# Another order of the seven half-size products in a fused sigmoid-attention and gated feed-forward kernel, with a second relu buffer and transposes in single banks

## The chip, the cores and the metric

The kernel runs on one core of a Trainium2 chip. The metric is the device time of one execution in microseconds (us), the median of several. A core has a matrix engine (TensorE, "PE" in the profile, with its weight loads shown apart as "PEld"), three engines for elementwise work (VectorE "DVE", ScalarE "ACT", GpSimd "POOL"), and DMA queues ("SPq" is the one that SyncE issues). TensorE writes its results to PSUM, here eight banks of 512 fp32 values for each of 128 partitions. This kernel uses four of the banks as two "pairs" (for attention) and four as single "banks" (for the feed-forward part).

## The reference, cut to what matters

```python
# q, k, v: (8, 12, 448, 64) fp32     w_gate, w_val: (768, 1536)     w_out: (1536, 768)
scores = q @ k.T / 8 - log(448)
attn   = sigmoid(scores) @ v                        # no softmax: each score alone
x      = attn, heads side by side                   # (3584 tokens, 768)
out    = (relu(x @ w_gate) * (x @ w_val)) @ w_out   # (3584, 768) fp32
```

There are 8 batches of 448 tokens. The kernel works on the feed-forward part of batch b and, woven into it, on the attention of batch b+1.

## The kernel before

For batches 1 to 7 the three matrix products are done by Winograd's form of Strassen's method: a product of 2 x 2 blocks costs seven block products in place of eight. For a group g of two feature blocks (six groups a batch) the products are numbered k = 1 to 7. Product 1, 2 and 4 take the tokens as they are (`xT`), products 3, 5, 6 and 7 take sums of token blocks (`S`); some of the weights are differences prepared before (`Tw`; for 7 the top half of `wv`, overwritten by a difference). One product is six matmuls of 128 x 128 by 128 x 224.

The seven products are put together in three banks: b1 holds 1, then adds 2; b2 holds 6, then adds 5, then adds 3; b3 holds 7, then adds 4. Between the products of one bank another engine reads what is there so far. A matmul that adds to a bank must therefore wait until the reader of the previous state is done.

```python
BANK = {1: "b1", 2: "b1", 6: "b2", 5: "b2", 3: "b2", 7: "b3", 4: "b3"}

def product(key, k, matmuls):
    first = k in (1, 6, 7)
    if first:
        live[key, BANK[k]] = take()            # the bank that was given back longest ago
    bank = banks[live[key, BANK[k]]]
    for i, (c0, c1, lhsT, rhs, last) in enumerate(matmuls):
        nc.tensor.matmul(bank[:, c0:c1], lhsT, rhs, start=(first and i == 0), stop=last, ...)

def tmp(key, nm):                              # s1, s2, s4: two buffers each; r1: one
    live[key, nm] = tmpp.tile([P, S], FP32, tag=nm, name=nm, bufs=1 if nm == "r1" else 2)
    return live[key, nm]

def gv_product(b, g, k):
    # ... the six matmuls, then, with ps = the bank:
    if k == 1:
        nc.scalar.copy(tmp(key, "s1")[:], ps)
    elif k == 6:
        add(tmp(key, "s2")[:], ps, live[key, "s1"][:])
    elif k == 5:
        t = tmp(key, "s4")
        add(t[:], ps, live[key, "s1"][:])
        add(t[:], banks[live[key, "b3"]][:, 0:S], t[:])
    elif k == 2:
        nc.scalar.activation(tmp(key, "r1")[:], ps, AF.Relu)
        give(i)
    elif k == 3:
        t = live[key, "s1"]
        add(t[:], ps, t[:])
        give(i)
        nc.gpsimd.tensor_tensor(out=out[:, :, o : o + HS], in0=two(live[key, "r1"]), in1=two(t), op=AOP.mult)
    elif k == 4:
        t = live[key, "s2"]
        add(t[:], ps, t[:])
        give(i)
        nc.vector.scalar_tensor_tensor(out=out[:, :, o + HS : o + S], in0=two(t), scalar=0.0,
            in1=two(live[key, "s4"]), op0=AOP.max, op1=AOP.mult)
```

`add` and `subtract` are VectorE `tensor_tensor` instructions. `out` is the activation tile `hT`. The last matrix product (`out_product`) works in the same way on pairs of token blocks (six matmuls of 128 x 384), with `hT` and sums of it as stationary operand. `sums(("h", pair), ks)` and `sums(("x", b), ks)` make the sums `S` on VectorE.

The order in which the products are emitted is a list; each engine executes its own instructions in the order of emission:

```python
def ffn(b):
    p, o = 4 * (b - 1), 4 * (b - 1) + 2        # the two pairs of output blocks of this turn
    todo = gv((0, 1)) if b == 1 else []        # each entry is (group, k)
    todo += gv((0, 7), (0, 2), (0, 6), (1, 1), (0, 5), (1, 6), (0, 3), (0, 4), (1, 7), (1, 5), (1, 2), (2, 1), (1, 3))
    for g in range(2, HFC):                    # HFC = 6
        todo += gv((g, 6), (g - 1, 4), (g, 7), (g, 5), (g, 2))
        todo += gv((g + 1, 1)) if g + 1 < HFC else [("out", p, 1)] if b > 1 else []
        todo += gv((g, 3))
    todo += gv((HFC - 1, 4))
    # ... then the output products; "plain" (b == 1) is an ordinary product of two token blocks
    # behind[...]: sums emitted straight after an entry
```

Attention is woven in by "visits": `scores(n, c)` makes two banks of a pair (four matmuls of 64 x 64 by 64 x 448), ScalarE turns them into one `PT` tile by a sigmoid, and `values(n, ...)` multiplies the seven `PT` tiles of a block of four heads by v. A visit is two scores, or score, values, score. The list `due` gives the times, counted in matmul time of the list, after which the next visit is emitted.

```python
PTp = ctx.enter_context(tc.tile_pool(name="PTp", bufs=9))

def transposes(n, nm, *engines, cut=(0, NCH)):
    if n <= NBLK:                              # NBLK = 3 blocks a batch, NCH = 7 chunks a block
        bank = take(); tr = banks[bank][:, 0:S]
    else:
        bank = None; tr = next_pair()[:, 0, 0:S]
    # ... seven PE transposes into tr, a copy to qT or kT, give(bank) if it was a bank

due = dues(0.5 if b > 1 else 1.5, total - 4.2) if b + 1 < B else []
```

On GpSimd run, in this order before batch 1: the casts of q, k and v of coming blocks, of the gate and value weights, and (as their DMAs land) of the twelve parts of `w_out` (`wo`).

Of the kernel before, what the change touches and what calls it, by code (L numbers as in the profile page):

```python
# [9 lines left out]
FP32 = mybir.dt.float32  # L10
FP16 = mybir.dt.float16
# [5 lines left out]
def kernel(  # L17
# [33 lines left out]
    h16p = ctx.enter_context(tc.tile_pool(name="h16p", bufs=3))  # L51
    v16p = ctx.enter_context(tc.tile_pool(name="v16p", bufs=3))
    qkTp = ctx.enter_context(tc.tile_pool(name="qkTp", bufs=4))
    PTp = ctx.enter_context(tc.tile_pool(name="PTp", bufs=9))
    xTp = ctx.enter_context(tc.tile_pool(name="xTp", bufs=4))
    sxp = ctx.enter_context(tc.tile_pool(name="sxp", bufs=1))
    tmpp = ctx.enter_context(tc.tile_pool(name="tmpp", bufs=2))
# [9 lines left out]
    def next_pair():  # L67
        turn["pair"] ^= 1
        return pairs[turn["pair"]]

    def take():

        return free.pop(0)

    def give(i):
        free.append(i)
# [98 lines left out]

    def transposes(n: int, nm: str, *engines, cut=(0, NCH)):
        h16 = qk16.pop((nm, n))
        if n <= NBLK:
            bank = take()
            tr = banks[bank][:, 0:S]  # L180
        else:
            bank = None
            tr = next_pair()[:, 0, 0:S]
        tr = tr.bitcast(FP16).rearrange("p (c h k) -> p c h k", c=NCH, h=2)
        for c in range(cut[0], cut[-1]):
            nc.tensor.transpose(tr[:, c], h16[:, c, :, :], ident[:])
        t2 = qkT.get((nm, n)) or qkTp.tile([P, NCH, 2, KC], FP16, tag="qkT", name=f"{nm}T")
        for c0, c1, eng in zip(cut, cut[1:], engines or (nc.vector,)):
            if eng is nc.scalar:
                eng.copy(t2[:, c0:c1], tr[:, c0:c1])  # L190
            else:
                eng.tensor_copy(t2[:, c0:c1], tr[:, c0:c1])
        if bank is not None:
            give(bank)
        qkT[nm, n] = t2

    def scores(n: int, c: int):
# [122 lines left out]
    def add(out, a, b):  # L320
        nc.vector.tensor_tensor(out=out, in0=a, in1=b, op=AOP.add)  # L321
# [69 lines left out]
    live: dict = {}  # L391

    def tmp(key, nm):
        live[key, nm] = tmpp.tile([P, S], FP32, tag=nm, name=nm, bufs=1 if nm == "r1" else 2)
        return live[key, nm]

    BANK = {1: "b1", 2: "b1", 6: "b2", 5: "b2", 3: "b2", 7: "b3", 4: "b3"}
# [12 lines left out]
    def gv_product(b: int, g: int, k: int):  # L410

        key = ("gv", b, g)
        h, kh = {1: (0, 0), 2: (0, 1), 4: (1, 1)}.get(k, (None, None))
        if h is None:
            a = [S_[("x", b), {3: 4, 5: 1, 6: 2, 7: 3}[k]][:, dc] for dc in range(HDC)]
        else:
            a = [xT[b, kh][:, dc, h * HS : (h + 1) * HS] for dc in range(HDC)]

        def w(j, dc):
            if k in (1, 2):  # L420
                return wg[j][:, (k - 1) * HDC + dc]
            if k == 3:
                return wv[j][:, HDC + dc]
            return T[{4: 4, 5: 1, 6: 2, 7: 3}[k], j][:, dc]

        mm = []
        for fi in range(2):
            j, jj = divmod(2 * g + fi, FG)
            for dc in range(HDC):
                mm.append((fi * HS, (fi + 1) * HS, w(j, dc)[:, jj * P : (jj + 1) * P], a[dc], dc == HDC - 1))  # L430
        product(key, k, mm)
        i = live[key, BANK[k]]
        ps = banks[i][:, 0:S]
        o = (b % NHALF) * S
        out = hT[:, 2 * g : 2 * g + 2]

        def two(t):
            return t[:].rearrange("p (f s) -> p f s", f=2)
# [5 lines that stand above are left out]
        elif k == 5:  # L444
            t = tmp(key, "s4")
            add(t[:], ps, live[key, "s1"][:])
            add(t[:], banks[live[key, "b3"]][:, 0:S], t[:])
        elif k == 2:
            nc.scalar.activation(tmp(key, "r1")[:], ps, AF.Relu)  # L449
            give(i)  # L450
        elif k == 3:
            t = live[key, "s1"]
            add(t[:], ps, t[:])
            give(i)
            nc.gpsimd.tensor_tensor(  # L455
                out=out[:, :, o : o + HS], in0=two(live[key, "r1"]), in1=two(t), op=AOP.mult
            )
        elif k == 4:
            t = live[key, "s2"]
            add(t[:], ps, t[:])  # L460
            give(i)
            nc.vector.scalar_tensor_tensor(  # L462
                out=out[:, :, o + HS : o + S],
                in0=two(t),
                scalar=0.0,
                in1=two(live[key, "s4"]),
                op0=AOP.max,
                op1=AOP.mult,
            )

    def out_product(pair: int, k: int):

# [84 lines left out]
    def ffn(b: int):  # L557


        p, o = 4 * (b - 1), 4 * (b - 1) + 2  # L560
        gv = lambda *gk: [("gv", b, *x) for x in gk]
        todo = gv((0, 1)) if b == 1 else []
        todo += gv((0, 7), (0, 2), (0, 6), (1, 1), (0, 5), (1, 6), (0, 3), (0, 4), (1, 7), (1, 5), (1, 2), (2, 1), (1, 3))
        for g in range(2, HFC):
            todo += gv((g, 6), (g - 1, 4), (g, 7), (g, 5), (g, 2))

            todo += gv((g + 1, 1)) if g + 1 < HFC else [("out", p, 1)] if b > 1 else []
            todo += gv((g, 3))
        todo += gv((HFC - 1, 4))
        behind = {("out", o, k): [] for k in (6, 5, 3)}  # L570
        end = ("gv", b, HFC - 1)
        nxt = [("gv", b + 1, 0, 1)] if b + 1 < B else []
        if b == 1:
            todo += ["plain"] + [("out", o, k) for k in (1, 2, 6, 5)] + nxt + [("out", o, k) for k in (7, 3, 4)]
            behind[*end, 4] = [(("h", o), [3, 2, 1, 4])]
            behind["out", o, 7] = [(("x", 2), [3, 2, 1])]
        else:
            todo += [("out", p, k) for k in (7, 2, 6)] + [("out", o, 1), ("out", p, 5), ("out", o, 2), ("out", p, 3)]
            todo += [("out", o, 7), ("out", o, 6), ("out", p, 4), ("out", o, 5)] + nxt + [("out", o, 3), ("out", o, 4)]

            early = b < 5
            behind[*end, 5] = [(("h", p), [3, 2, 1] if early else [3])]
            behind[*end, 3] = [(("h", p), [4])] if early else []
            behind[*end, 4] = [] if early else [(("h", p), [2, 1, 4])]
            behind["out", p, 6] = [(("h", o), [3])]
            behind["out", p, 5] = [(("h", o), [2])]
            behind["out", p, 3] = [(("h", o), [1, 4])]
            if nxt:
                behind["out", o, 6] += [(("x", b + 1), [3])]
                behind["out", o, 5] += [(("x", b + 1), [2, 1])]  # L590
        if nxt:
            behind["out", o, 3] += [(("x", b + 1), [4])]
        return todo, behind
# [60 lines left out]
    def dues(first, last):  # L654

        work = [sum(1.2 if what == "v" else 1.0 for what, _ in x) for x in visits]
        at = [0.0]
        for x, w in zip(visits, work):
            if x[0][0] == "v":
                break  # L660
            at.append(at[-1] + w)
        return [first + a / at[-1] * (last - first) for a in at]
# [9 lines left out]
    with tc.manual_schedule():  # L672
# [109 lines left out]
        for b in range(1, B):  # L782
            todo, behind = ffn(b)
            plain_us = 2 * NFC * (DM / 2400.0 + 0.004)
            us = lambda x: plain_us if x == "plain" else GV_US if x[0] == "gv" else OUT_US
            total = sum(us(x) for x in todo)
            due = dues(0.5 if b > 1 else 1.5, total - 4.2) if b + 1 < B else []
            t = 0.0
            for x in todo:
                if x == "plain":  # L790
                    t1 = t
                    for block in range(2):
                        for cost in out_plain(block):
                            t1 += cost
                            if due and t1 >= due[0]:
                                due.pop(0)
                                visit()
                            if late_out and t1 - t >= (7 - len(late_out)) * 1.1:
                                late_out.pop(0)()
                    assert not late_out  # L800
                    out_weights(3, 0)
                else:
                    one(x, behind)
                t += us(x)
                if due and t >= due[0] and (x[0] == "out" or x[-1] in (2, 6, 7)):
                    due.pop(0)
                    visit()
                    if late:
                        late.pop(0)()
            assert not due and not late  # L810
# [29 lines left out]
```

## Time and profile before

| | |
|---|---|
| Time, median of 3 runs | 423.74 us (423.56 to 425.36) |
| Span of the profiled execution | 423.2 us |
| PE busy | 400.5 us, 95% |
| DVE busy | 284.3 us, 67% |
| ACT busy | 235.4 us, 56% |
| POOL busy | 170.1 us, 40% |
| Mean granted TensorE clock | 0.991 |

The profile page gives the busy time of each engine, and the span in 40 slices. The list of waits says which engine waited for which, in total, how often, and the longest. The timeline gives instructions in order of time: start, duration, engine, line of the kernel, operation, output and inputs, count, and in brackets the idle time of that engine just before and what ended it. Matmuls overlap one another in their records (a matmul of 224 columns has a record of about 260 ns but the next begins about 96 ns later), so a busy PE can hide small waits; these are read from the starts of successive products. The first 68 us hold the attention of batch 0 and the feed-forward part of batch 0 (not in Strassen's form); then each batch takes about 50 us.

### The profile page before, as it was taken

Reading aid. Unit: us, or ns where it says so; the run is one execution under the profiler, and the core shown is the slowest. Engines: PE = TensorE matmul, PEld = TensorE weight load, DVE = VectorE, ACT = ScalarE, POOL = GpSimd, SP = SyncE. Lnnn points to the kernel's source line nnn. Section 1 sums busy time; section 2 is a strip of 40 time slices with the busy share of each in tenths; the row PEclk is TensorE's granted clock in tenths of the full one; section 3 lists DMA queues with packets and bytes.
Section 4 is the critical chain, followed back from the end, with each engine's and each line's share of the span. In section 5 each row is a group of like instructions: output and inputs, shape, how many; then the busy total and the mean of one; then the engine's idle time right before and its main releaser. Section 6 shows DMA issues by size and latency. Waiting matters only on the chain.

```text
span 423.2 us, 9597 instructions
## 1 busy us (share of the span) xinstructions
PE 400.5 (95%) x3946; PEld 277.0 (65%) x3946; DVE 284.3 (67%) x464; ACT 235.4 (56%) x332; POOL 170.1 (40%) x187
## 2 busy tenths in 40 slices
PE   7889999699999999999999999999999999999994
PEld 3344446487557785677756786578855788568952
DVE  3444776667947776576765777576876677658883
ACT  5957775357445675556744665646755567532120
POOL 2677857834412544054340636115550252102310
PEclk9999999889999999999999999999999999999999
DMA  8999969464087626476255755476363950041006
GB/s 297 384 384 384 356 164 395 118 169 132 7 243 182 172 74 175 110 213 175 48 166 126 176 161 133 118 138 161 128 173 77 205 90 2 2 107 43 2 0 150
DMA packets 64476, 67.08 MB, mean 158 GB/s; under 512 B 35888, under 2 KB 54832, under 8 KB 64432
## 3 DMA queue, kind: packets, MB, share of 16 engines
q1 hardware_dynamic: 63184, 64.53, 53.1%
q10 hardware_dynamic: 1248, 1.93, 1.4%
q8 instruction: 31, 0.51, 0.5%
q14 instruction: 13, 0.11, 0.1%
HBM read 47.19 MB, written 11.01 MB: 138 GB/s over the span
## 4 chain that ended last, share of the span: by engine, by line
PE 70%; DMA 14%; DVE 8%; POOL 3%; issue 2%; SPq 2%; ACT 1%; DVEq 0%; ACTq 0%; POOLq 0%
PE bank L406 55%; PE pair L202 7%; DMA st_wu<-in_moe_w_val_dram 6%; PE pair L231 6%; DVE s L321 5%; DMA st_wo<-in_moe_w_out_dram 3%; DMA st_q<-in_q_dram 3%; DMA st_v<-in_v_dram 2%; PE bank L541 2%; POOL wo L164 1%; SPq L111 1%; DVE hT L462 1%; DVE s L492 1%; POOL h16k L133 1%; POOL wv L157 0%
## 5 line engine op out<-in xcount | busy, mean ns | idle before, releaser
L212 ACT ACTIVATE PT<-pair,bias_t 128x896 f16<-128x896 f32 x168 | 160.8, 1014 | 69.9 <-PE pair L202 69.8
L321 DVE TENSOR_TENSOR s<-bank,s 128x448 f32<-128x448 f32 x210 | 126.6, 620 | 63.9 <-PE bank L406 58.3
L455 POOL TENSOR_TENSOR hT<-r,s 128x448 f16<-128x448 f32 x42 | 48.2, 1147 | 187.7 <-DVE s L321 169.2
L406 PEld LDWEIGHTS <-Tw 128*128 128x128 f16 x756 | 71.4, 99 | 16.0 <-issue 14.8
L406 PE MATMUL bank<-S,wv 128*128 128x224 f16 x504 | 62.6, 260 | 3.9 <-DVE s L321 2.8
L406 PE MATMUL bank<-S,Tw 128*128 128x224 f16 x504 | 62.1, 262 | 4.2 <-ACT r L449 2.7
L406 PE MATMUL bank<-xT,wg 128*128 128x224 f16 x504 | 59.8, 260 | 0.0
L202 PE MATMUL pair<-qT,kT 64*64 64x448 f16 x672 | 54.3, 366 | 5.0 <-ACT PT L212 3.4
L406 PEld LDWEIGHTS <-wv 128*128 128x128 f16 x504 | 48.4, 98 | 8.6 <-issue 7.5
L406 PEld LDWEIGHTS <-wg 128*128 128x128 f16 x504 | 47.2, 98 | 6.7 <-issue 5.7
L449 ACT ACTIVATE r<-bank 128x448 f32<-128x448 f32 x42 | 22.8, 543 | 47.4 <-PE bank L406 44.3
L406 PEld LDWEIGHTS <-S 128*128 128x128 f16 x312 | 29.0, 98 | 27.5 <-issue 8.0
L202 PEld LDWEIGHTS <-kT 64*64 64x64 f16 x672 | 17.9, 104 | 31.9 <-issue 26.4
L462 DVE SCALAR_TENSOR_TENSOR hT<-s,s 128x448 f16<-128x448 f32 x42 | 37.4, 891 | 1.4
L492 DVE SCALAR_TENSOR_TENSOR s<-bank,s 128x384 f32<-128x384 f32 x26 | 14.5, 557 | 30.8 <-PE bank L406 29.3
L249 ACT ACTIVATE xT<-pair 128x448 f16<-128x448 f32 x42 | 20.5, 541 | 21.4 <-PE pair L231 21.3
L406 PEld LDWEIGHTS <-hT 128*128 128x128 f16 x234 | 22.8, 98 | 14.7 <-issue 0.4
L406 PE MATMUL bank<-To,S 128*128 128x384 f16 x156 | 29.7, 327 | 2.5 <-DVE S L321 1.8
L406 PE MATMUL bank<-xT,Tw 128*128 128x224 f16 x252 | 31.7, 262 | 0.0
L231 PE MATMUL pair<-PT,v 64*64 64x448 f16 x588 | 31.5, 350 | 0.0
L406 PE MATMUL bank<-wo,S 128*128 128x384 f16 x156 | 29.3, 326 | 1.0 <-DVE s L492 0.6
L406 PE MATMUL bank<-wo,hT 128*128 128x384 f16 x156 | 29.6, 326 | 0.1
(71 smaller groups left out, 408.8 us busy)
## 6 DMA issues: line engine op xcount, KB each, us to landing
st_q<-in_q_dram SPq DMA_DIRECT2D x23, 448.0 KB, 4.7
st_v<-in_v_dram SPq DMA_DIRECT2D x23, 448.0 KB, 5.4
out_dram<-ysb SPq DMA_DIRECT2D x53, 192.0 KB, 2.7
st_k<-in_k_dram SPq DMA_DIRECT2D x22, 448.0 KB, 4.1
st_wg<-in_moe_w_gate_dram SPq DMA_DIRECT2D x6, 768.0 KB, 11.9
st_wu<-in_moe_w_val_dram SPq DMA_DIRECT2D x6, 768.0 KB, 12.3
st_wo<-in_moe_w_out_dram SPq DMA_DIRECT2D x12, 384.0 KB, 5.9
st_v<-in_v_dram ACTq DMA_DIRECT2D x1, 448.0 KB, 5.6
```

Of the source, the lines that this page charges most:

```text
L111: eng.dma_start(st[:, :, c0 * D : c1 * D], rows[:, :, c0 * D : c1 * D])
L202: nc.tensor.matmul(ps[o : o + 64, bank, 0:S], kT[r : r + 64, c, h, :], qT[r : r + 64, :, h, :], start=True, stop=True, tile_position=(r, o ...
L212: nc.scalar.activation(pt[:], ps[:, :, 0:S], AF.Sigmoid, bias=bias_t[:], scale=qk_scale)
L231: nc.tensor.matmul(pv[pr][o : o + 64, 0:S], t[r : r + 64, pr, c * D : (c + 1) * D], pt[r : r + 64, pr, :], start=(c == 0), stop=(c == NCH ...
L249: nc.scalar.activation(x, pv[pr][:, 0:S], AF.Copy, scale=XSCALE)
L321: nc.vector.tensor_tensor(out=out, in0=a, in1=b, op=AOP.add)
L406: nc.tensor.matmul(bank[:, c0:c1], lhsT, rhs, start=(first and i == 0), stop=last, skip_group_check=True)
L449: nc.scalar.activation(tmp(key, "r1")[:], ps, AF.Relu)
L455: nc.gpsimd.tensor_tensor(out=out[:, :, o : o + HS], in0=two(live[key, "r1"]), in1=two(t), op=AOP.mult)
L462: nc.vector.scalar_tensor_tensor(out=out[:, :, o + HS : o + S], in0=two(t), scalar=0.0, in1=two(live[key, "s4"]), op0=AOP.max, op1=AOP.mult,)
L492: nc.vector.scalar_tensor_tensor(out=out, in0=ps, scalar=OUT_SCALE, in1=c, op0=AOP.mult, op1=AOP.add)
L541: nc.tensor.matmul(banks[i][:, 0:mn], hT[:, f, o : o + P], wo[:, f, m0 : m0 + mn], start=(f == 0), stop=(f == NFC - 1))
```

## The change

- The first group of each batch: (0, 5) is emitted straight after (0, 6), before (1, 1); and (1, 5) before (1, 7). The first visit of a batch falls later in the list (1.5 in place of 0.5; in batch 1, 2.0 in place of 1.5).
- The second addition into `s4`, which needs product 7 in b3 and product 5 in b2, is emitted after whichever of the two comes last, and no longer always with product 5.
- `r1`, the relu's output, has two buffers instead of one; the `PT` tiles pay for it with eight buffers instead of nine.
- The transposes of q and k of blocks 4 and 5 take a single bank, as those of the blocks before do, and not a half of a pair.
- In batches 5 to 7 the gate-times-value multiplication of the last group, whose result the output product needs at once, is done on VectorE instead of GpSimd, and the sums behind it are spread: sum 2 straight after it, sums 1 and 4 after (5, 4).
- Batch 1: output product 1 of pair 2 stands between (5, 2) and (5, 3) (other batches had one there already), and the remaining output products run 6, 2, 7, 5, 3, 4 instead of 2, 6, 5, 7, 3, 4.

It is meant to give the readers of each bank more time before the next product needs the bank, and to keep a late multiplication on GpSimd from holding up the next relu.

```diff
-    PTp = ctx.enter_context(tc.tile_pool(name="PTp", bufs=9))
+    PTp = ctx.enter_context(tc.tile_pool(name="PTp", bufs=8))
@@ transposes
-        if n <= NBLK:
-            bank = take()
-            tr = banks[bank][:, 0:S]
-        else:
-            bank = None
-            tr = next_pair()[:, 0, 0:S]
+        bank = take()
+        tr = banks[bank][:, 0:S].bitcast(FP16).rearrange(...)
...
-        if bank is not None:
-            give(bank)
+        give(bank)
@@ tmp
-        live[key, nm] = tmpp.tile([P, S], FP32, tag=nm, name=nm, bufs=1 if nm == "r1" else 2)
+        live[key, nm] = tmpp.tile([P, S], FP32, tag=nm, name=nm)
@@ gv_product
         elif k == 5:
             t = tmp(key, "s4")
             add(t[:], ps, live[key, "s1"][:])
-            add(t[:], banks[live[key, "b3"]][:, 0:S], t[:])
...
-            nc.gpsimd.tensor_tensor(
-                out=out[:, :, o : o + HS], in0=two(live[key, "r1"]), in1=two(t), op=AOP.mult
-            )
+            eng = nc.vector if g == HFC - 1 and b >= 5 else nc.gpsimd
+            eng.tensor_tensor(out=out[:, :, o : o + HS], in0=two(live[key, "r1"]), in1=two(t), op=AOP.mult)
...
+        if k in (5, 7) and (key, "s4") in live and (key, "b3") in live:
+            t = live[key, "s4"]
+            add(t[:], banks[live[key, "b3"]][:, 0:S], t[:])
@@ ffn
-        todo += gv((0, 7), (0, 2), (0, 6), (1, 1), (0, 5), (1, 6), (0, 3), (0, 4), (1, 7), (1, 5), (1, 2), (2, 1), (1, 3))
+        todo += gv((0, 7), (0, 2), (0, 6), (0, 5), (1, 1), (1, 6), (0, 3), (0, 4), (1, 5), (1, 7), (1, 2), (2, 1), (1, 3))
...
-            todo += gv((g + 1, 1)) if g + 1 < HFC else [("out", p, 1)] if b > 1 else []
+            todo += gv((g + 1, 1)) if g + 1 < HFC else [("out", p if b > 1 else o, 1)]
...
-            todo += ["plain"] + [("out", o, k) for k in (1, 2, 6, 5)] + nxt + [("out", o, k) for k in (7, 3, 4)]
+            todo += ["plain"] + [("out", o, k) for k in (6, 2, 7, 5)] + nxt + [("out", o, k) for k in (3, 4)]
...
-            behind["out", o, 7] = [(("x", 2), [3, 2, 1])]
+            behind["out", o, 5] = [(("x", 2), [3, 2, 1])]
...
-            behind[*end, 3] = [(("h", p), [4])] if early else []
-            behind[*end, 4] = [] if early else [(("h", p), [2, 1, 4])]
+            behind[*end, 3] = [(("h", p), [4] if early else [2])]
+            behind[*end, 4] = [] if early else [(("h", p), [1, 4])]
@@ the loop over the batches
-            due = dues(0.5 if b > 1 else 1.5, total - 4.2) if b + 1 < B else []
+            due = dues(1.5 if b > 1 else 2.0, total - 4.2) if b + 1 < B else []
```

`early` is `b < 5`; `end` is the last group of the batch. Up to batch 4 the pair `p` needs no activation of the batch in hand; from batch 5 on it does.

## The prediction

> **What bounds the kernel now.** I read the page first (busy shares and the row of the granted clock), then the list of PE's waits, then the windows of ten microseconds, then the timeline where the waits lie. Page:
>
> ```profile
> PE 400.5 (95%) x3946; PEld 277.0 (65%) x3946; DVE 284.3 (67%) x464; ACT 235.4 (56%) x332; POOL 170.1 (40%) x187
> ```
>
> PE is the bound: no other engine is over 67%. So only what shortens or removes a stall of PE counts. The waits and the window with the low clock:
>
> ```profile
> PE bank L406 <- DVE s L321: 4.3, 15, 0.5
> PE bank L406 <- ACT r L449: 2.7, 1, 2.7
> PE bank L406 <- DVE S L321: 1.8, 3, 0.9
> ...
> 80.00:90.00 10.00, 7.97 (x70) 5.17 (x70) 5.10 (x7) 4.31 (x6) 5.19 (x7) 0.66 0.71 186
> ```
>
> Three kinds of stall: many short ones behind additions, one long one behind a relu, three behind sums. The window says that the clock fell to 0.66 on average where the long one lies. The long one in the timeline:
>
> ```profile
> 79.39 0.93 POOL L133 CAST h16k<-st_k 128x896 f16<-128x896 f32 x1
> 80.28 1.12 POOL L455 TENSOR_TENSOR hT<-r,s 128x448 f16<-128x448 f32 x1
> 81.44 0.54 ACT L449 ACTIVATE r<-bank 128x448 f32<-128x448 f32 x1 [3.08 <-POOL hT L455]
> 81.88 0.53 ACT L441 COPY s<-bank 128x448 f32<-128x448 f32 x1
> 82.03 1.28 PE L406 MATMUL bank<-S,Tw 128*128 128x224 f16 x6 [2.73 <-ACT r L449]
> ...
> 85.23 1.33 PE L406 MATMUL bank<-S,wv 128*128 128x224 f16 x6
> 86.35 1.33 PE L406 MATMUL bank<-S,Tw 128*128 128x224 f16 x6
> ```
>
> GpSimd is late with casts of `wo`, whose DMAs it awaits, so group 0's multiplication ends at 81.40; only then is the one `r1` free, so the relu of (1, 2) comes at 81.44, and (2, 6), which takes that relu's bank, at 82.03. After it products start 86.35 - 85.23 = 1.12 us apart, against 0.58 below: half clock, until about 88. The start of an ordinary batch (batch 3):
>
> ```profile
> 178.93 0.74 PE L406 MATMUL bank<-S,Tw 128*128 128x224 f16 x6
> 179.51 0.74 PE L406 MATMUL bank<-xT,wg 128*128 128x224 f16 x6
> 180.46 1.31 PE L406 MATMUL bank<-S,Tw 128*128 128x224 f16 x12 [0.21 <-DVE s L321]
> ...
> 183.63 0.73 PE L406 MATMUL bank<-S,wv 128*128 128x224 f16 x6 [0.33 <-DVE s L321]
> 184.29 0.57 PE L202 MATMUL pair<-qT,kT 64*64 64x448 f16 x8
> ```
>
> 178.93 is (0, 6), 179.51 is (1, 1): a product takes 0.58 us. (0, 5) starts 1.53 after (0, 6), of which 0.95 is drain plus one 0.62 us addition. (1, 7) comes at 183.63. Against a steady 0.58, (0, 5), (0, 3) and (1, 7) lose 0.37, 0.30 and 0.49: 1.16 us a batch, seven times. And the end of batch 5:
>
> ```profile
> 311.03 1.14 POOL L455 TENSOR_TENSOR hT<-r,s 128x448 f16<-128x448 f32 x1 [3.73 <-DVE s L321]
> 311.45 1.20 DVE L462 SCALAR_TENSOR_TENSOR hT<-s,s 128x448 f16<-128x448 f32 x1
> 312.57 0.90 DVE L321 TENSOR_TENSOR S<-hT,S 128x768 f16<-128x768 f16 x1
> 313.40 0.91 DVE L321 TENSOR_TENSOR S<-hT 128x768 f16<-128x768 f16 x1
> 313.54 1.15 PE L406 MATMUL bank<-To,S 128*128 128x384 f16 x6 [0.85 <-DVE S L321]
> ```
>
> Output product 6 waits for sum 2, which stands behind the last multiplications. By the starts this costs 1.02, 0.65 and 0.61 us in batches 5, 6 and 7.
>
> **What the Trainium skill says.** "TensorE: Matmul & The Clock Gate", Part 1, says that TensorE runs at half clock after about one idle window of 3.4 us and needs a busy one to come back; its closing table advises no idle gap over about 3 us. The trace roughly agrees: one gap of 2.73 us was followed by some 6 us at doubled pitch, while the gaps of 0.5 us were not. "Perfetto Trace Analysis", Identifying Performance Opportunities, says that consistent bubbles can mean that there are not enough buffers for the next tile: here the 1.16 us a batch are that for PSUM banks. "SBUF — State Buffer", Who interferes with whom, says that VectorE and GpSimd share a port pair by an exclusive lock: the `scalar_tensor_tensor` above takes 1.20 us beside GpSimd's multiplication; elsewhere it is 0.62 (75.86 in the timeline).
>
> **Part 1, the start of a batch (2 to 6).** The old order puts one product between (0, 6) and (0, 5). The new one puts none, but the later first visit falls exactly there: walking the list against 1.5 us, (0, 7), (0, 2), (0, 6) make 1.73. With (0, 7) at 177.18 as now: (0, 2) 177.76, (0, 6) 178.33, visit 179.00 to 179.51, (0, 5) at 178.33 + 1.53 = 179.86, a loss of 0.35. Then (1, 1) 180.44, (1, 6) 181.01, (0, 3) 181.59 (its addition is done by 181.39), (0, 4) 182.17, (1, 5) 182.74, (1, 7) 183.32 (bank free at about 183.27, so just in time), second visit 183.98 against 184.29 now. But there is now one product less between this visit and (2, 6), and (2, 6) takes the bank of (1, 2), whose relu stands on ScalarE behind the visit's two sigmoids (about 0.95 us pitch each). Today (2, 6) comes 187.12 - 184.29 = 2.83 after the visit with the relu just ended; so in the new order at 186.81, where 0.51 + 3 x 0.58 would give 186.2. So 0.35 + 0.6 is lost in place of 1.16 and some 0.1 at turns: third visit 187.47 against 187.78. **Gain 0.3 us a batch**, five times, and about 0.25 in batch 7, which has no visits: **1.8 us.**
>
> **Part 2, batch 1.** The casts on GpSimd follow the DMAs, not PE, so I leave group 0's multiplication at 80.28 to 81.40. With two `r1` the relu of (1, 2) no longer waits; by the walk of part 1, (2, 6) starts at about 78.6. The next copy of ScalarE, (2, 1) into `s1`, still does: `s1` has two buffers, and group 0's is read by that same multiplication. So the copy runs to 81.95, addition (2, 6) to 82.6, and (2, 5) starts at 82.66, where PE would want it at 80.96. The stall moves one step and shrinks from 2.9 to 1.7 us. Then (2, 2), the visit, and (3, 1) at 86.1 in place of 90.32 if the clock holds: 4.2 us. If the clock still falls, the doubled pitch (0.55 + 0.38 + 1.6 + 0.2 = 2.7 us today) is paid again: 1.5 us. I give that one in four: **3.5 us** on average. Behind it, output product 1 fills the 0.66 us that (5, 3) loses at 104.89, and order 6, 2, 7, 5 puts two products and a visit between 6 and 5, which today loses 0.88 at 121.01; product 3 then has only 0.58 + 0.98 us behind 5 where 1.86 is needed and loses 0.3. **1.2 us.**
>
> **Part 3, the ends of batches 5 to 7.** Two VectorE additions (1.15), then the multiplication (0.62 as for the additions, my estimate) and sum 2 (0.59): sum 2 is ready about 2.0 us after the first addition starts, where today it takes 3.2, and product 6 wants it at 2.25. So product 6 waits no more. But VectorE now carries 0.62 us more: the rest (addition, `scalar_tensor_tensor`, two sums, the reader of 6) ends near 5.0, and output product 5 waits for it. Batch 6: product 5 wants 4.86 in place of 5.5 today, gain 0.5; batch 7 without a visit 4.2, so 5.0 against 4.87 today: nothing; batch 5, with sums of 0.9 us beside GpSimd, 0.3. **0.8 us.**
>
> **Part 4, eight PT buffers.** In one visit per batch the score is the ninth live tile: its sigmoid must wait until the first values matmuls have read the oldest. These start one group of four (0.2 us) after the score, so the sigmoid is 0.2 us later, and the second score of that visit waits for it (in batch 5 the sigmoid ends at 309.04 and that score starts at 309.09). **Loss 7 x 0.2 = 1.3 us.**
>
> **Part 5, transposes and later additions.** PE's waits for pairs (3.4 us in 10 times) are behind sigmoids, not transposes; four banks are enough beside gate and value. **0.** The split addition is the same instruction elsewhere, and is in part 1.
>
> Sum: 1.8 + 3.5 + 1.2 + 0.8 - 1.3 = 6.0 us: 417.7. With the clock held, the likelier case, 6.7: 417.0. I say **417.4 us.**
>
> **Rivals.** (a) The reorder only swaps one wait for another: the relu behind the sigmoids gives back all of part 1, or the 0.6 us grows. For it speaks that old and new are within 0.3 us by my own walk; it would give 419. (b) The half clock comes even with 1.7 us of stall: 420 with nothing else changed. For it, the fall came before the 2.73 us gap was over, so less than 3 us suffices. (c) GpSimd's multiplication is not as fixed as I take it, (2, 5) hardly waits, and the ninth-tile wait hides in slack: 2 us more from batch 1 and 1 us from part 4, 414. (d) VectorE becomes the bound at the batch ends: it is 85% busy in the window 310 to 320, and a queue there would cost 1 us.
>
> **Range and chances.** Parts 1, 3 and 4 are sums of differences of 0.2 to 0.6 us repeated five to seven times, uncertain by about 1 us each; the clock is a step of 2.7. Eight in ten: 414.2 to 420.4. Faster by over 2% means below 415.3: 0.15. Slower by over 2% would need a new stall in every batch: 0.01. Within 2%: 0.84.
>
> **What would show it.** The clock of the window 80 to 90 near 1.0 and PE waiting for `s` and not for `r` there (part 2); (0, 5) about 1.53 after (0, 6) with a visit between and (2, 6) following a relu in each batch (part 1); PE's waits for sums gone and a wait for an output addition in their place (part 3); a second score of one visit per batch late by 0.2 (part 4). A low clock as today, or new waits for `r` of over 1 us a batch, would make it wrong upwards; batches of under 49 us where they take 50, downwards.

## The result, and the profile after

| | before | after |
|---|---|---|
| Time, median | 424.55 us (423.56 to 426.65, 4 runs) | 420.24 us (419.81 to 420.47, 4 runs) |
| Ratio after to before | | 0.989 (95% interval 0.985 to 0.993) |
| Span of the profiled execution | 423.2 us | 418.6 us |

The changed kernel is 1.1% faster. PE is still the bound; of the page's first part:

```profile
PE 397.4 (95%) x3946; PEld 276.6 (66%) x3946; DVE 284.7 (68%) x467; ACT 237.6 (57%) x332; POOL 167.0 (40%) x184
```

PE's waits (in total, times, the longest), and the window of ten microseconds with the low clock (stretch, sum, then each engine's busy time, the granted clock, DMA):

```profile
PE bank L400 <- DVE s L315: 5.5, 9, 2.8
PE pair L196 <- ACT PT L206: 3.4, 10, 0.7
PE bank L400 <- ACT r L442: 2.6, 6, 0.5
...
PE bank L400 <- DVE ysb L489: 0.5, 1, 0.5
```

```profile
80.00:90.00 10.00, 7.16 (x61) 4.15 (x60) 5.59 (x7) 4.92 (x8) 5.57 (x7) 0.66 0.68 180
```

The one wait of 2.7 us for the relu `r` has become one of 2.8 us for an addition `s`; the relu now holds PE up six times for up to 0.5 us; the waits for sums (`S`) are gone; the clock still falls to 0.66 in the same window.

Where the time went is best seen by stages, each measured in the trace from the start of (0, 7) in one batch to that in the next; batch 1 is cut at (3, 1):

| us | batch 1 to (3, 1) | batch 1 from (3, 1) | 2 | 3 | 4 | 5 | 6 |
|---|---|---|---|---|---|---|---|
| before | 21.63 | 36.91 | 49.95 | 49.95 | 49.95 | 50.97 | 50.42 |
| after | 20.99 | 35.68 | 50.48 | 49.75 | 49.75 | 49.75 | 49.56 |
| gained | 0.64 | 1.23 | -0.53 | 0.20 | 0.20 | 1.22 | 0.86 |

These add up to 3.8 us. Batch 7 and the end give 0.25 more (44.78 and 44.53). The remaining 0.53 us lies ahead of batch 1 (68.69 and 68.16), and I do not credit it to the change: kernels below that are the same as the changed one up to there start batch 1 between 67.95 and 68.57. The first column does not repeat: four kernels below that are the same as the changed one through it take 19.90, 20.42, 20.66 and 20.79 us there, so its 0.64 stands for anything from 0.6 to 1.7. The second repeats within 0.1 us where the slow clock ends before it (35.61 in two of them); where the slow clock reaches well into it, it was 36.76.

**The first group of batch 1.** The timeline of the changed kernel:

```profile
80.02 0.93 POOL L133 CAST h16k<-st_k 128x896 f16<-128x896 f32 x1
80.92 1.12 POOL L450 TENSOR_TENSOR hT<-r,s 128x448 f16<-128x448 f32 x1
82.07 0.53 ACT L435 COPY s<-bank 128x448 f32<-128x448 f32 x1 [4.14 <-POOL hT L450]
82.64 0.62 DVE L315 TENSOR_TENSOR s<-bank,s 128x448 f32<-128x448 f32 x1 [4.26 <-ACT s L435]
83.31 1.28 PE L400 MATMUL bank<-S,Tw 128*128 128x224 f16 x6 [2.84 <-DVE s L315]
84.39 1.32 PE L400 MATMUL bank<-xT,wg 128*128 128x224 f16 x6
85.64 0.59 PE L196 MATMUL pair<-qT,kT 64*64 64x448 f16 x4
```

The chain that was predicted stands there link by link: the multiplication of group 0 on GpSimd, the copy of (2, 1) into the `s1` that it frees, addition (2, 6), and (2, 5) on PE. It is only longer: PE is ready for (2, 5) some 0.5 us sooner than I had it, and the multiplication ends 0.64 us later (82.04, not 81.40). The pitch of 1.08 us from 83.31 to 84.39 is the half clock.

**The start of an ordinary batch** (batch 3):

```profile
176.46 0.74 PE L400 MATMUL bank<-S,Tw 128*128 128x224 f16 x6
177.13 0.57 PE L196 MATMUL pair<-qT,kT 64*64 64x448 f16 x8
177.99 0.73 PE L400 MATMUL bank<-S,Tw 128*128 128x224 f16 x6 [0.28 <-DVE s L315]
...
182.10 0.57 PE L196 MATMUL pair<-qT,kT 64*64 64x448 f16 x8
182.54 1.90 ACT L206 ACTIVATE PT<-pair,bias_t 128x896 f16<-128x896 f32 x2 [2.63 <-PE pair L196]
184.33 0.54 ACT L442 ACTIVATE r<-bank 128x448 f32<-128x448 f32 x1
184.93 0.73 PE L400 MATMUL bank<-S,Tw 128*128 128x224 f16 x6 [0.42 <-ACT r L442]
```

(0, 5) starts 1.53 us after (0, 6), with the visit between them; (2, 6) starts 2.83 after the second visit and just behind the relu, whose two predecessors on ScalarE are that visit's sigmoids. Where nothing waits, a visit starts 0.67 us after a product, and the next product 0.50 us after a visit of two scores. So (0, 5) loses 1.53 - 1.17 = 0.36 us; (2, 6) starts 1.16 us after (1, 3) in place of 0.58 and loses 0.58.

**The end of batch 5:**

```profile
307.81 0.63 DVE L315 TENSOR_TENSOR s<-bank,s 128x448 f32<-128x448 f32 x1 [2.14 <-PE bank L400]
...
308.54 0.62 DVE L450 TENSOR_TENSOR hT<-r,s 128x448 f16<-128x448 f32 x1
309.27 0.56 DVE L315 TENSOR_TENSOR S<-hT,S 128x768 f16<-128x768 f16 x1
...
310.06 1.14 PE L400 MATMUL bank<-To,S 128*128 128x384 f16 x6
310.39 0.63 DVE L455 SCALAR_TENSOR_TENSOR hT<-s,s 128x448 f16<-128x448 f32 x1
310.94 0.55 DVE L315 TENSOR_TENSOR S<-hT 128x768 f16<-128x768 f16 x1
...
311.87 0.55 DVE L489 SCALAR_TENSOR_TENSOR s<-bank,s 128x384 f32<-128x384 f32 x1
```

Sum 2 is ready at 309.83 and output product 6 no longer waits. What stood at 1.20 and 0.9 us on VectorE before takes 0.63 and 0.55 now.

**The start of batch 2**, the one stage that lost:

```profile
124.91 1.23 DVE L315 TENSOR_TENSOR S<-xT 128x672 f16<-128x672 f16 x1
126.06 0.55 DVE L489 SCALAR_TENSOR_TENSOR ysb<-bank,s 128x384 f32<-128x384 f32 x1
126.66 0.73 PE L400 MATMUL bank<-S,Tw 128*128 128x224 f16 x6 [0.52 <-DVE ysb L489]
```

(0, 6) takes the bank of output product 3 of batch 1, whose reader stands on VectorE behind sum 1 of the next `x`: 0.68 us by the starts.

### The profile page after: what moved, and what is told of

It is laid out like the page before. It is cut to its first block, busy times and chain, and to the rows that moved or that the text cites. A ratio compares the mean times of both kernels' runs of the same rounds, so it can differ in the third digit from the quotient of the medians.

```text
span 418.6 us, 9648 instructions
## 1 busy us (share of the span) xinstructions
PE 397.4 (95%) x3946; PEld 276.6 (66%) x3946; DVE 284.7 (68%) x467; ACT 237.6 (57%) x332; POOL 167.0 (40%) x184
## 3 DMA queue, kind: packets, MB, share of 16 engines
q10 hardware_dynamic: 1248, 1.93, 1.3%
## 4 chain that ended last, share of the span: by engine, by line
PE 77%; DMA 9%; DVE 6%; POOL 3%; issue 1%; ACT 1%; SPq 1%; ACTq 0%; DVEq 0%
PE bank L400 57%; PE pair L196 8%; PE pair L225 7%; DMA st_wu<-in_moe_w_val_dram 3%; PE bank L263 3%; DMA st_wo<-in_moe_w_out_dram 3%; DMA st_k<-in_k_dram 2%; DVE s L315 2%; PE bank L538 2%; POOL wo L164 1%; DVE s L489 1%; DVE S L315 1%; POOL h16k L133 1%; ACT PT L206 1%; ACT r L442 1%
## 5 line engine op out<-in xcount | busy, mean ns | idle before, releaser
L450 POOL TENSOR_TENSOR hT<-r,s 128x448 f16<-128x448 f32 x39 | 45.2, 1159 | 173.2 <-DVE s L315 108.8
L400 PE MATMUL bank<-S,Tw 128*128 128x224 f16 x504 | 62.6, 260 | 8.4 <-DVE s L315 5.3
L455 DVE SCALAR_TENSOR_TENSOR hT<-s,s 128x448 f16<-128x448 f32 x42 | 36.1, 860 | 1.4
L225 PE MATMUL pair<-PT,v 64*64 64x448 f16 x588 | 32.9, 361 | 0.0
L133 POOL CAST h16q<-st_q 128x896 f16<-128x896 f32 x21 | 20.3, 968 | 30.5 <-DMA st_q<-in_q_dram 23.2
```

Source lines behind the costliest of these rows:

```text
L133: eng.tensor_copy(o, i)
L225: nc.tensor.matmul(pv[pr][o : o + 64, 0:S], t[r : r + 64, pr, c * D : (c + 1) * D], pt[r : r + 64, pr, :], start=(c == 0), stop=(c == NCH ...
L450: eng.tensor_tensor(out=out[:, :, o : o + HS], in0=two(live[key, "r1"]), in1=two(t), op=AOP.mult)
```

## The experiments

Each kernel is the changed kernel with one edit, except the mended kernel, which has four. Ratios are to the kernel before, run on the same chip; the changed kernel's own is 0.989.

| kernel | median, us | ratio (95%) |
|---|---|---|
| group 0's multiplication on VectorE | 421.41 | 0.991 (0.988 to 0.994) |
| second visit after (1, 2) | 416.82 | 0.982 (0.979 to 0.986) |
| one relu buffer, nine PT tiles | 421.20 | 0.990 (0.987 to 0.993) |
| old order of the first groups | 421.41 | 0.992 (0.989 to 0.995) |
| half of w_out later | 414.97 | 0.977 (0.976 to 0.979) |
| last multiplications back on GpSimd | 421.94 | 0.995 (0.993 to 0.997) |
| sum 1 of batch 2's x later | 419.42 | 0.988 (0.986 to 0.990) |
| the mended kernel | 410.60 | 0.967 (0.965 to 0.970) |
| sums of the batch ends together (one run) | 422.30 | |
| old order of batch 1's output products (one run) | 420.87 | |

Batches 3 to 6 repeat within 0.02 us from kernel to kernel where nothing touches them (batches 3 and 4: 49.75), so effects of 0.1 us are read from these stages, not from the medians. Batch 1 up to (3, 1) scatters by 1.1 us (19.90 to 20.99 in kernels that are the same there), and the medians of the kernel before on the chips used are 424.55 to 425.17, so differences of that size in that stage, or of 0.6 us between medians, decide nothing.

### The multiplication out of GpSimd's queue: a theory that fell

```diff
-            eng = nc.vector if g == HFC - 1 and b >= 5 else nc.gpsimd
+            eng = nc.vector if (g == HFC - 1 and b >= 5) or (b == 1 and g == 0) else nc.gpsimd
```

> The changed kernel, with the gate-times-value multiplication of group 0 of batch 1 on VectorE instead of GpSimd; nothing else. Theory: the stall that the second relu buffer only moved (2.84 us before (2, 5), then half clock) comes from that one multiplication standing behind late casts on GpSimd, because the copy into s1 waits for it, and the clock falls only because of the stall. Then the stall and the low clock in the window 80 to 90 both vanish: 2.9 us of stall and about 2.6 of slow matmuls, 5.5 us, 414.8 in the median. Rival 1: the next multiplication in the same queue (group 1, at 84.62) takes over and stalls the copy of group 3: less than 2.5 us gained. Rival 2: the clock falls there whatever PE does: 2.9 us gained, the clock still 0.66 in that window.

Nothing was gained: 421.41 us. The stall before (2, 5) is indeed gone, but PE then stands still at the next visit, and the clock of the window 80 to 90 is 0.83. Timeline:

```profile
80.41 1.65 POOL L133 CAST h16k<-st_k 128x896 f16<-128x896 f32 x1
82.09 1.23 SPq L171 DMA_TRANSPOSE kT<-h16k  x1
83.36 1.30 SPq L171 DMA_TRANSPOSE qT<-h16q  x1
86.47 0.46 PE L196 MATMUL pair<-qT,kT 64*64 64x448 f16 x4 [4.85 <-DMA qT<-h16q]
```

The visit's first score is the first of block 7, and it needs that block's k and q. K is cast on GpSimd at 80.41; its transpose by DMA starts at 82.09, that of q stands behind it at 83.36, and the score waits for q until about 86.4. In the changed kernel the same score starts at 85.64, straight after the delayed (2, 5) and (2, 2). So two walls stand at about the same time, both made by the same queue: behind the last casts of `wo` on GpSimd come the k cast of block 7 and the multiplication. Neither theory I had put down named this; rival 1 was right that something else in that queue takes over.

### Half of the w_out casts later: the cause

```diff
         nc.sync.dma_start(flat, moe_w_out[f * P : (f + 1) * P, :])
-        eng.tensor_copy(wo[:, f], flat)
+        if f < 6:
+            eng.tensor_copy(wo[:, f], flat)
+        else:
+            late_cast.append(lambda: eng.tensor_copy(wo[:, f], flat))
...
+                    if b == 1 and x[2:] in [(1, 2), (2, 1), (1, 3), (2, 6), (1, 4), (2, 7)]:
+                        start_next()                      # loads part 6 and on
+                    if b == 1 and x[2:] in [(3, 1), (2, 3), (3, 6), (2, 4), (3, 7), (3, 5)]:
+                        late_cast.pop(0)()
```

> The changed kernel with the last six of the twelve parts of w_out loaded and cast later: their loads after (1, 2) to (2, 7) of batch 1, their casts on GpSimd six products later; they are needed only some 25 us after that. New theory: the wall near 86 us is not the multiplication but GpSimd's queue of casts paced by the w_out DMAs: the k cast of block 7 stands in it, then its DMA transpose, then the first score of block 7, and the multiplication in the same queue is a second victim that happens to hold PE up to the same time. With half of the w_out casts out of the way both come 4 us or more earlier: no stall over 0.7 us in the first group of batch 1, the clock 1.00 in the window 80 to 90, (3, 1) near 83.8 instead of 89.15: 5.3 us, 414.9. Rival: block 7 itself is late from memory (its own loads), then the stall before its first score stays and at most 1 us is gained.

414.97 us: 5.3 less than the changed kernel, as expected. Batch 1 up to (3, 1) takes 15.37 us in place of 20.99. Timeline and the window:

```profile
73.41 0.93 POOL L133 CAST h16k<-st_k 128x896 f16<-128x896 f32 x1
74.31 1.13 POOL L456 TENSOR_TENSOR hT<-r,s 128x448 f16<-128x448 f32 x1
74.36 1.23 SPq L177 DMA_TRANSPOSE kT<-h16k  x1
...
81.52 0.38 PE L202 MATMUL pair<-qT,kT 64*64 64x448 f16 x4
```

```profile
80.00:90.00 10.00, 10.00 (x123) 8.34 (x121) 9.04 (x14) 5.96 (x11) 7.38 (x8) 1.00 1.18 350
```

Cast and multiplication come 6.6 us sooner, block 7's first score starts without a wait, the clock stays at 1.00 and PE is busy all through the window. What this edit moves is only when six parts of `w_out` are loaded and cast (the loops that start loads before batch 1, not shown, stop ahead of them); so the wall was their place ahead of block 7's casts and the multiplication. The rival, that block 7's own loads are late, is out: in the changed kernel its k and q have landed by 62.6 and 63.8 us. GpSimd's queue there:

```profile
66.06 8.02 POOL L164 CAST wo<-st_wo 128x768 f16<-128x768 f32 x8 [7.82 <-DMA st_wo<-in_moe_w_out_dram]
75.33 0.83 POOL L164 CAST wo<-st_wo 128x768 f16<-128x768 f32 x1 [1.25 <-DMA st_wo<-in_moe_w_out_dram]
76.10 0.93 POOL L133 CAST h16q<-st_q 128x896 f16<-128x896 f32 x1
76.98 3.09 POOL L164 CAST wo<-st_wo 128x768 f16<-128x768 f32 x3
```

Whether it is more the wait for the loads or the time of the casts was not tried apart, and this trace leaves it open: the last six casts take 5.7 us themselves, but the last load lands only at 78.2.

### One relu buffer and nine PT tiles

```diff
-    PTp = ctx.enter_context(tc.tile_pool(name="PTp", bufs=8))
+    PTp = ctx.enter_context(tc.tile_pool(name="PTp", bufs=9))
-        live[key, nm] = tmpp.tile([P, S], FP32, tag=nm, name=nm)
+        live[key, nm] = tmpp.tile([P, S], FP32, tag=nm, name=nm, bufs=1 if nm == "r1" else 2)
```

> The changed kernel with one relu buffer and nine PT tiles, as before the change. Theory: the second relu buffer is worth about 2.5 us in batch 1 (without it (2, 6) waits from 77.4 to about 82.6, and the work between (2, 6) and (2, 5) comes after the stall and at half clock: (3, 1) near 91.6 instead of 89.15), and nothing later; eight PT tiles cost 0.15 us in one visit per batch, so batches 3 and 4 take 49.6 instead of 49.75: together about 1.6 us slower, 421.8. Rival: with the stall where GpSimd puts it in either case the second buffer is worth nothing, and nine PT tiles give 0.8 us: 419.4.

Batches 3 and 4 take 49.61 and 49.62: nine tiles are worth 0.14 us a batch, as expected. Batch 1 up to (3, 1) takes 22.45 us, so by this one trace the second relu buffer is worth 1.5 to 2.5 us there (against 20.99 in the changed kernel, and 19.90 to 20.79 in those that are the same up to there); the expected 2.5 is at the end of that range. With the tiles' loss, about 0.85, that leaves 0.6 to 1.7 us net over the kernel; the medians are 1.0 apart. The relu waits here for 4.57 us, and PE with it:

```profile
82.41 0.54 ACT L442 ACTIVATE r<-bank 128x448 f32<-128x448 f32 x1 [4.57 <-POOL hT L450]
...
83.00 1.28 PE L400 MATMUL bank<-S,Tw 128*128 128x224 f16 x6 [5.11 <-ACT r L442]
```

In the visit of batch 5 with the ninth tile, the changed kernel's timeline shows where the 0.14 goes:

```profile
304.95 0.38 PE L196 MATMUL pair<-qT,kT 64*64 64x448 f16 x4
...
305.58 1.01 ACT L206 ACTIVATE PT<-pair,bias_t 128x896 f16<-128x896 f32 x1
...
306.63 0.38 PE L196 MATMUL pair<-qT,kT 64*64 64x448 f16 x4
```

The sigmoid starts 0.63 us after the score and the second score 1.68 after the first; with nine tiles these are 0.50 and 1.55 (306.23, 306.73 and 307.78 in that trace).

### The old order of the first groups

```diff
-        ... (0, 6), (0, 5), (1, 1), (1, 6), (0, 3), (0, 4), (1, 5), (1, 7), (1, 2), ...
+        ... (0, 6), (1, 1), (0, 5), (1, 6), (0, 3), (0, 4), (1, 7), (1, 5), (1, 2), ...
-            due = dues(1.5 if b > 1 else 2.0, total - 4.2) if b + 1 < B else []
+            due = dues(0.5 if b > 1 else 1.5, total - 4.2) if b + 1 < B else []
```

> The changed kernel with the old order of the first two groups and the old times of the first visit; everything else of the change stays. Theory: the new order is worth about 0.37 us in batches 3 to 6 (1.26 of stalls before, 0.89 after), nothing in batch 1, where the wait for GpSimd absorbs it, nothing in batch 7, and minus 0.3 in batch 2, where the later visit leaves (0, 6) waiting 0.68: about 1.2 us slower, 421.4. Rival: one wait was swapped for another of the same size: 420.2, with batches 3 and 4 at 49.75 as before.

Batches 3 to 5 take 50.09 and batch 6 49.90: the new order is worth 0.34 us in each. Batch 2 takes 50.15, 0.33 less, and batch 7 with the end 44.58, 0.05 more. Batch 1 up to (3, 1) takes 20.60, within what kernels with the new order show there, so no effect is shown. The stages make 1.1 us, and the median, 421.41, is 1.2 us up, as expected; the rival is out.

### The second visit after the relu

```diff
-                if due and t >= due[0] and (x[0] == "out" or x[-1] in (2, 6, 7)):
+                if due and t >= due[0] and (x[0] == "out" or (x[-1] in (2, 6, 7) and x[2:] != (1, 7))):
```

> The changed kernel, with the second visit of each batch after (1, 2) instead of after (1, 7). Theory: (2, 6) waits 0.58 us a batch because the relu of (1, 2), which frees its bank, stands on ScalarE behind the visit's two sigmoids. With the relu in front of them this wait goes: 0.58 us in batches 2 to 6, in batch 1 nothing as the later stall absorbs it: 2.9 us, 417.3 in the median. Rival: the copy of (2, 1) into s1 now stands behind the sigmoids and holds up addition (2, 6) and so (2, 5): at most 0.1 us a batch, 419.8.

416.82 us, 3.4 less. Batches 3 to 5 take 49.17 in place of 49.75. Timeline of batch 3:

```profile
181.10 0.54 ACT L442 ACTIVATE r<-bank 128x448 f32<-128x448 f32 x1 [2.87 <-PE bank L400]
...
181.54 1.90 ACT L206 ACTIVATE PT<-pair,bias_t 128x896 f16<-128x896 f32 x2
...
182.66 0.74 PE L400 MATMUL bank<-S,Tw 128*128 128x224 f16 x6
```

The relu now stands ahead of the sigmoids and (2, 6) has no wait. The copy of (2, 1) does come behind the sigmoids, as the rival said, but (2, 5) is late enough in the list not to mind.

### Sum 1 of the next x after output product 3

```diff
-            behind["out", o, 5] = [(("x", 2), [3, 2, 1])]
+            behind["out", o, 5] = [(("x", 2), [3, 2])]
-            behind["out", o, 3] += [(("x", b + 1), [4])]
+            behind["out", o, 3] += [(("x", b + 1), [1, 4] if b == 1 else [4])]
```

> The changed kernel with sum 1 of batch 2's x emitted after output product 3 together with sum 4, instead of after output product 5. Theory: (0, 6) of batch 2 waits 0.68 us for the bank of output product 3, whose reader stands on VectorE behind sum 1; with sum 1 later the wait goes, and batch 2 takes 49.75 like batches 3 and 4, down from 50.48: 0.7 us, 419.5. Rival: (0, 5), which needs sum 1, waits in its place: no change, 420.2.

Batch 2 takes 49.95 in place of 50.48, a gain of 0.53. The wait of (0, 6) is gone; that of (0, 5) grows from 0.36 to 0.49, a little of what the rival said. The median, 419.42, agrees with 419.5.

### The ends of batches 5 to 7, two ways

```diff
-            eng = nc.vector if g == HFC - 1 and b >= 5 else nc.gpsimd
+            eng = nc.gpsimd
```

> The changed kernel with the last group's multiplication of batches 5 to 7 back on GpSimd; the spread sums stay. Theory: that move to VectorE is what shortened batches 5, 6 and 7 (by 1.0, 0.65 and 0.15 us besides the rest), because sum 2 no longer waits for GpSimd[...]: batches 5 and 6 get back 0.65 us or more each, as sum 2 now even stands in front of addition (5, 4): 1.5 to 2.5 us slower, 422.2. Rival: the spreading of the sums did it: within 0.3 us of the changed kernel.

Batch 5 takes 50.70 and batch 6 49.89: 0.95 and 0.33 us back, in batch 6 less than the 0.65 expected; batch 7 with the end takes 45.16, 0.63 back where 0.15 was expected. The median is 1.7 up. Sum 2 waits for GpSimd again, and addition (5, 4) behind it (timeline, batch 5):

```profile
309.88 1.13 POOL L450 TENSOR_TENSOR hT<-r,s 128x448 f16<-128x448 f32 x1 [3.83 <-ACT PT L206]
...
311.04 0.88 DVE L315 TENSOR_TENSOR S<-hT,S 128x768 f16<-128x768 f16 x1 [1.31 <-POOL hT L450]
...
311.98 1.15 PE L400 MATMUL bank<-To,S 128*128 128x384 f16 x6 [0.45 <-DVE S L315]
```

```diff
-            behind[*end, 3] = [(("h", p), [4] if early else [2])]
-            behind[*end, 4] = [] if early else [(("h", p), [1, 4])]
+            behind[*end, 3] = [(("h", p), [4])] if early else []
+            behind[*end, 4] = [] if early else [(("h", p), [2, 1, 4])]
```

> The changed kernel with the sums behind the last group of batches 5 to 7 as before (2, 1 and 4 together after (5, 4)); the multiplication stays on VectorE. Theory: both halves of that part are needed: with addition (5, 4) and its 0.63 us of scalar_tensor_tensor in front of sum 2 again, sum 2 is ready 0.47 + 0.6 us later than the 2.0 us after the first addition of the changed kernel, so output product 6 waits about 0.8 us, and batches 5 and 6 take 50.4 and 50.2 instead of 49.75 and 49.56. Rival: the multiplication's move alone did it: 49.75 and 49.56 stay.

Batches 5 and 6 take 50.58 and 50.39, output product 6 waits 0.82 us in each. That is 0.83 us back in either batch, near the 0.65 expected. So in batch 5 both halves of this part are needed; in batch 6 the spread sums alone keep half of the gain (0.33 us).

### The old order of batch 1's output products

```diff
-            todo += gv((g + 1, 1)) if g + 1 < HFC else [("out", p if b > 1 else o, 1)]
+            todo += gv((g + 1, 1)) if g + 1 < HFC else [("out", p, 1)] if b > 1 else []
-            ... [("out", o, k) for k in (6, 2, 7, 5)] + nxt + [("out", o, k) for k in (3, 4)]
-            behind["out", o, 5] = [(("x", 2), [3, 2, 1])]
+            ... [("out", o, k) for k in (1, 2, 6, 5)] + nxt + [("out", o, k) for k in (7, 3, 4)]
+            behind["out", o, 7] = [(("x", 2), [3, 2, 1])]
```

> The changed kernel with the output products of batch 1 in the old order (1 after the plain product, then 2, 6, 5, 7, 3, 4). Theory: the new order took 1.2 us out of the second part of batch 1, from (3, 1) to the start of batch 2, and 0.68 us of that came back as the wait of (0, 6) in batch 2, so the undone kernel needs 1.2 us more in batch 1 and 0.5 to 0.7 less in batch 2, 0.6 us more in all. Rival: the second part of batch 1 is bound by VectorE's queue of weight differences, and the order changes nothing there: batch 2 alone is 0.7 shorter.

Batch 1 from (3, 1) takes 37.61 us, 1.93 more; the stalls of 0.66 and 0.88 are back, and a further one of 0.43 at 93.48 lies before any of the moved products and is not this edit's. Batch 2 takes 49.75, 0.73 less. So the new order gains 1.5 us in batch 1 and pays 0.7 of it in batch 2.

### The mended kernel

The edits of "half of w_out later", "second visit after (1, 2)", "sum 1 later" and "one relu buffer, nine tiles" together.

> The changed kernel with all of these: w_out's last six parts later, second visit after (1, 2), sum 1 of batch 2's x later, and one relu buffer with nine PT tiles as before the change. Theory: the second relu buffer only served a queue that is no longer late, so one is enough, and nine PT tiles save 0.14 us a batch. Sum: 5.3 for the wall, 0.58 x 6 for the visit, 0.7 for the sum, 0.85 for the tiles: 10.3 us off 420.2, 409.9, and no wait over 1 us between 60 and 370. Rival: with one relu buffer a relu waits for GpSimd again, which would show as a wait for r of over 1 us in batch 1, 412.

410.60 us, 3.3% faster than before. PE's waits:

```profile
PE pair L202 <- ACT PT L212: 3.9, 11, 0.7
PE bank L406 <- DVE s L321: 2.8, 8, 0.8
```

No wait of PE is put down to a relu. But in batch 1 the relu of (1, 2) does wait for GpSimd, as the rival said, and PE feels it one step later:

```profile
74.90 1.50 POOL L456 TENSOR_TENSOR hT<-r,s 128x448 f16<-128x448 f32 x1
76.43 0.54 ACT L448 ACTIVATE r<-bank 128x448 f32<-128x448 f32 x1 [3.62 <-POOL hT L456]
78.82 0.38 PE L202 MATMUL pair<-qT,kT 64*64 64x448 f16 x4 [0.51 <-ACT PT L212]
```

The relu starts 1.50 us after its product, where it takes 0.77 with two buffers (second visit after (1, 2), batch 1). The sigmoids behind it are late by as much, and from the next visit's start to the next product it takes 1.21 us, against 0.54 in batch 3. So with GpSimd's queue in order one buffer still costs about 0.7 us, once, a little less than the 0.85 that nine tiles bring; it would account for the 0.7 us by which the kernel misses the expected 409.9. A kernel with the other mends, two buffers and eight tiles was not run. Batches 3 to 5 take 49.07.

## Why the prediction was right or wrong

The time, 420.24, lies near the upper end of the range; the predicted 417.4 was 2.8 us too low. That it lies inside is partly luck: part 2 with its cost in batch 2 brought 3.5 us less than predicted, parts 3 and 4 together some 1.3 us more.

- **Part 1, the start of a batch** (0.3 us each): right, step by step. Stalls of 0.35 and 0.6 were predicted; they are 0.36 and 0.58. The old order costs 0.34 us a batch more. Only batch 7 was wrong: with no visit between, (0, 5) loses 0.95 us there, and the old order costs 0.05 and not 0.25.
- **Part 2, batch 1 up to (3, 1)** (3.5 us on average, 4.2 if the clock holds): wrong, 0.64 in the two traces. Two steps failed. The first: "the stall moves one step and shrinks from 2.9 to 1.7 us". It moved and did not shrink (2.84), since PE comes sooner and GpSimd later than I had put them; and with it the clock fell, the case that I gave one in four. The second: "then (2, 2), the visit, and (3, 1) at 86.1". That visit's first score needs block 7's k and q, and in the eight kernels with two relu buffers and that queue of casts it starts between 85.64 and 86.47, whatever PE waited for before; from that score to (3, 1) it takes 2.0 us even at full clock (81.52 to 83.50 in the kernel with half of w_out later). So at full clock (3, 1) would have come at about 87.6 (my estimate: 85.64 + 1.98), 1.5 us after the predicted 86.1, and the half clock brought it to 89.15, another 1.5 us. I had looked at what PE waited for, and not at what the next piece would wait for if this were gone. With the stall taken away, (3, 1) still came at 89.85; with the queue mended, at 83.50. Rival (b), that the clock falls even with 1.7 us of stall, is likelier than I had it: in the kernel with the old order, gaps of 1.83 us before (2, 5) and 0.73 before the score were enough.
- **Part 2, the rest of batch 1** (1.2): right, 1.23; but "product 3 then loses 0.3" was the smaller price. The larger one, 0.68 us in batch 2 behind sum 1, I had not seen: I had checked when each sum is ready and not who waits behind it on VectorE.
- **Part 3, the ends of batches 5 to 7** (0.8): the mechanism right, the size too small. Net of the other parts, batch 5 gained 1.22 - 0.20 = 1.0 and batch 6 0.86 - 0.20 = 0.7 us where I had 0.3 and 0.5. The term that was off is the rest of VectorE's work: I put its end at 5.0 us after the first addition, and 0.9 us on each sum in batch 5; in the trace it ends at about 4.6 (312.42 - 307.81), with sums of 0.55, since GpSimd is idle there from 306.7. Two readings were also off: the terms given for sum 2 add up to 2.36 and not 2.0 (one addition stands ahead of the multiplication, not two; measured 2.02), and product 6 of batch 7 loses 0.65 before the change, not 0.61.
- **Part 4, eight tiles** (1.3 lost, though 7 x 0.2 is 1.4): right in kind, 0.14 a batch in place of 0.2.
- **Part 5, transposes** (0): not tried alone. Ahead of batch 1 a wait of 0.54 us for qT at 50.32 stands where the kernel before has 0.13 and 0.15; the 0.53 us gained there is within what equal kernels show.

## What to carry to other kernels

Before a stall is credited with its length, ask what the work behind it waits for: here two walls from one GpSimd queue stood about a microsecond apart, and taking one away brought nothing, while moving six loads and casts that are needed much later took both. A buffer added in front of a late engine moved the wait to the next buffer of the same reader; putting the engine's queue in order removed most of it (about 0.7 us, once, was left to the single buffer). A stage whose time scatters between equal kernels has to be known as such before a difference in it is read. Where several engines run in order, it pays to place short instructions that free a bank ahead of long ones (the relu ahead of two sigmoids: 0.58 us a batch), and this costs only a place in a list.

## What the runs showed of the hardware

- The slow stretch of TensorE's clock came in two lengths. In the window 80 to 90 a mean of 0.66 means 6.8 us at half (before, after), and the 0.83 in the kernel with group 0's multiplication on VectorE means 3.4 us, although there PE stood still for 4.85 us, longer than the 2.73 and 2.84 of the other two. Nor is it the code: of the five kernels that are the same up to there, two had 6.8 us (stalls of 2.84 and 2.91) and three 3.4 us (2.90, 2.96 and 3.58). So the length of a stall did not set the length of the slow stretch. The two lengths fit the free-running windows of some 3.4 us that the Trainium skill describes ("TensorE: Matmul & The Clock Gate", Part 1). A gap well under one window was enough: the 2.73 us before, less than the 3 us that the page's closing table advises to stay under. Runs of one kernel differ as well: of 18 runs of the kernel before, three had a mean clock of 0.998 to 1.0 and took 422.2 to 422.4 us, the others 0.990 to 0.996 and 423.7 to 425.4.
- At the end of batch 5, VectorE instructions with both inputs in SBUF took 0.55 to 0.63 us when GpSimd was idle; before the change they took 1.20 us beside GpSimd's multiplication and 0.9 beside its casts of v. Moving the multiplication to VectorE, the busier engine, made VectorE's work there end sooner: 4.6 us after the first addition (312.42 - 307.81) in place of 5.35 (315.61 - 310.26). With the sums together again and only the multiplication moved, the instructions were as short (0.55 to 0.63).
